# DeltaNet and a SiLU feed-forward on one core: chunk 1's inverses placed by VectorE instead of through DRAM, and GpSimd turning rows in chunks 2 to 5

## The chip, the cores and the metric

The kernel runs on one core of one Trainium2 chip. The metric is device time in microseconds (us) of one execution. The kernel before takes 667.36 us, the median of three runs (666.45, 667.36 and 670.78).

## The reference

A linear-attention block (DeltaNet) feeds a two-layer feed-forward block. There are 4 batches, 8 heads, 768 tokens and a head width of 48. All of it is fp32.

```python
k_n = k / (norm(k, axis=-1) + 1e-06)
state = zeros((B, H, D, D))
for t in range(S):
    y[:, :, t] = einsum('bhd,bhde->bhe', q[:, :, t], state)
    v_old = einsum('bhde,bhd->bhe', state, k_n[:, :, t])
    state = state + beta[:, :, t] * einsum('bhd,bhe->bhde', k_n[:, :, t], v[:, :, t] - v_old)
x = y.transpose(0, 2, 1, 3).reshape(3072, 384)
h = x @ w_in                                   # 384 -> 2048
out = (h * (1.0 / (1.0 + exp(-h)))) @ w_out    # 2048 -> 384
```

## The kernel before, in words

**Tiling.** The 768 tokens are six chunks of 128 (c = 0 to 5), and a chunk has two halves of 64 tokens (hf). The 32 pairs of batch and head are handled together, in two groups g of 16. Within a half, the recurrence is a triangular system. Its 64x64 inverse is made of 32x32 inverses on the diagonal and a corner that joins two of them. One partition holds one 32x32 inverse, so the 128 inverses of a chunk (32 pairs, four blocks of 32 tokens) fill the 128 partitions.

**One chunk.** TensorE makes the scores (`score`, L502). `block_out` (L543) sends the 32x32 diagonal blocks to DRAM and `block_in` (L550) fetches them back with one block to a partition (tile `g`). `invert` (L569) runs 31 pairs of VectorE instructions (L580, L585) on tile `x` and one final scaling (L588). Then the inverses have to come back to token-major places. In the kernel before, chunks 1 to 5 do it through DRAM: ScalarE and VectorE each turn half the rows of 64 partitions into `g` (`turn_rows`, L573, through `by_act` and `by_dve`, L517 and L520), the SP queue writes `low` and `up` to DRAM, reads `low` back as `xe` (L600) and `up` back into `xi` and `crossed` (`read_up`, L556). Chunk 0 has a way of its own, `invert_first` (L613), with two VectorE 32x32 transposes (L640, L644).

**Joins.** `solve(c)` (L922) goes on in steps: `merge(c, g, False)` (TensorE L732, reads `xe`, writes `py`, evacuated to `y` by ScalarE and VectorE), `keys` (L778, then VectorE adds into `vf`, L783), `merge(c, g, True)` (L732 into `px`, reads `xi`, `crossed` and `y`), and then for each half `inner` and `old` (L790, L856), `update` (L810), `new` (L869), and `copy_out`, which copies results to `xT` and `part`; `move` (L847) issues five DMAs `xT<-part` for each half. The scaling of `vf` by the norms (`size`, L438) is a GpSimd instruction of 128x768.

**Feed-forward.** A generator yields pieces of the previous chunk's feed-forward: `hidden` (L985, `phid`, then SiLU on ScalarE into `gT`, L995), and `project` (L1015, `po`) for chunk 0, or `combine` (L1083) for the later chunks. `combine` needs sums of quarters of `w_out`, made once by `sum_w` (VectorE L1047, eight instructions). `run(n)` puts n pieces into the order; TensorE does them while the recurrence waits.

**Order.** `pin` (L76) chains every instruction of an engine to the one before it, so each engine executes in exactly the order in which the Python code emits. The SP queue likewise takes its DMAs in order (`in_line`, L86). How much feed-forward lies between two steps of the recurrence is written out by hand: `script` texts for chunk 0 (L1421), the loops after `invert(1, step)` (L1430 to L1439), and the tuple of counts in the main loop (L1445). Weights are narrowed while they come in (`narrow`, L213: two ScalarE, two VectorE, one GpSimd instruction for a piece); `fill` (L1179) advances that, and when `eager` is set it begins the next piece at once.

`place(c, j)` (L412) says which 32 partitions token block j takes: identity for chunk 0, permuted for the others. `spread` (L312) holds the norms in these places, zero elsewhere; it is set to zero once more at L1252.

## Time and profile before

| what | value |
|---|---|
| median of three runs | 667.36 us |
| the profiled execution | 669.8 us, of it the span of instructions 668.1 us |
| TensorE matmul busy | 638.2 us (96% of the span) |
| VectorE / ScalarE / GpSimd busy | 393.0 / 215.7 / 84.3 us |
| mean granted TensorE clock | 0.969 of full speed |
| packets of the main DMA queue | 40.7% of 16 engines' span |

The profile is of one execution. A busy TensorE counts the time that matmuls are in flight, at whichever clock was granted, so a busy microsecond at half clock does half the work. In the timeline each row is a start, a duration, the engine, the line in the kernel, the operation with its output and inputs, and how many instructions were merged into the row; in brackets stands how long the engine was idle before and what ended the idle time. One `Matmult` of fp32 appears as two matmuls in these rows. SPq is the SP engine's queue, on which the DMAs are issued.

### The profile page before, as it was taken

What the parts mean: (1) busy time and instruction counts of PE and PEld (TensorE: products, weight loads), DVE (VectorE), ACT (ScalarE), POOL (GpSimd) and SP (SyncE); (2) the same over time, 40 slices, a digit from 0 to 9 for tenths busy, and PEclk for the clock granted to TensorE, in tenths of its full rate; (3) what the DMA queues carried; (4) which work ended last, traced back from release to release, by engine and by line L of the source; (5) the groups of instructions that cost most, each with busy time, mean ns of one, the idle gap of its engine ahead of it and who ended that gap; (6) DMA issues with size and microseconds to landing.
All of it is one profiled execution on the core that took longest, in us unless ns stands there. A gap on an engine that the chain in (4) does not pass through costs nothing.

```text
span 668.1 us, 21115 instructions
## 1 busy us (share of the span) xinstructions
PE 638.2 (96%) x9288; PEld 554.7 (83%) x9288; DVE 393.0 (59%) x908; ACT 215.7 (32%) x496; POOL 84.3 (13%) x86
## 2 busy tenths in 40 slices
PE   7849998998989999999999999999999999999997
PEld 5547785685778998998988998989988989989997
DVE  6845797995455796562895462977553974212112
ACT  2435685112234112452122452122452122441111
POOL 5022483500102002002001002001011000000000
PEclk9956999998889999999999999999999999999999
DMA  8991737606055816065905066715073024010101
GB/s 133 215 260 35 238 104 176 107 0 106 13 117 110 135 26 104 4 125 113 137 24 104 10 130 132 108 37 93 12 148 86 1 72 58 16 37 1 25 0 25
DMA packets 153195, 56.39 MB, mean 84 GB/s; under 512 B 124480, under 2 KB 146240, under 8 KB 153104
## 3 DMA queue, kind: packets, MB, share of 16 engines
q1 hardware_dynamic: 150656, 54.63, 40.7%
q8 instruction: 73, 1.20, 0.8%
q10 hardware_dynamic: 2448, 0.41, 0.4%
q14 instruction: 18, 0.15, 0.1%
HBM read 41.06 MB, written 11.80 MB: 79 GB/s over the span
## 4 chain that ended last, share of the span: by engine, by line
PE 54%; DVE 21%; DMA 6%; SPq 3%; issue 2%; ACT 2%; POOL 0%; DVEq 0%; ACTq 0%
PE phid L985 20%; PE px L1083 11%; PE py L1083 9%; DVE rank L580 8%; DVE x L585 7%; PE pa L502 2%; PE pz L790 2%; DVE sums_of_g L1065 2%; SPq L100 2%; PE ph L778 2%; DMA g<-blocks 2%; PE pyc L869 2%; PE pu L810 1%; PE po L1015 1%; DMA blocks<-ap 1%
## 5 line engine op out<-in xcount | busy, mean ns | idle before, releaser
L985 PE MATMUL phid<-xT,w_in 128*128 128x256 f32 x1152 | 259.8, 383 | 5.1 <-ACT gT L995 3.0
L985 PEld LDWEIGHTS phid<-xT,w_in 128*128 128x128 f32 x1152 | 216.6, 191 | 38.4 <-issue 4.6
L995 ACT ACTIVATE gT<-phid 128x512 f32<-128x512 f32 x96 | 57.0, 597 | 146.1 <-PE phid L985 139.2
L580 DVE SCALAR_TENSOR_TENSOR rank<-g,step,x 128x31 f32<-128x31 f32 (+15 forms) x155 | 63.4, 409 | 41.6 <-DMA g<-blocks 37.2
L1065 DVE TENSOR_TENSOR sums_of_g<-gT 128x384 f32<-128x384 f32 (+1 forms) x60 | 29.8, 510 | 56.4 <-ACT gT L995 45.5
L585 DVE TENSOR_TENSOR x<-x,rank 128x31 f32<-128x31 f32 (+15 forms) x155 | 55.9, 361 | 5.3
L1083 PE MATMUL px<-sums_of_w,sums_of_g 128*128 128x192 f32 x320 | 56.1, 329 | 0.0
L1083 PE MATMUL py<-w_out,sums_of_g 128*128 128x192 f32 x320 | 56.1, 329 | 0.0
L1083 PEld LDWEIGHTS px<-sums_of_w,sums_of_g 128*128 128x128 f32 x320 | 52.1, 190 | 0.5
L1083 PEld LDWEIGHTS py<-w_out,sums_of_g 128*128 128x128 f32 x320 | 52.1, 190 | 0.4
L1015 PE MATMUL po<-w_out,gT 128*128 128x384 f32 x128 | 47.1, 519 | 2.3 <-ACT gT L995 2.1
L361 POOL TENSOR_TENSOR sq<-kb 128x384 f32<-128x384 f32 x24 | 21.6, 921 | 182.1 <-DMA low<-g 130.8
L1015 PEld LDWEIGHTS po<-w_out,gT 128*128 128x128 f32 x128 | 24.3, 198 | 19.4 <-ACT gT L995 2.8
L443 POOL TENSOR_TENSOR vf<-vf,n_slot 128x768 f32<-128x768 f32 x10 | 14.6, 1475 | 157.1 <-DMA vf<-in_v_dram 157.1
L464 DVE STREAM_TRANSPOSE kq<-stage 128x512 f32<-128x512 f32 x28 | 28.4, 1121 | 8.3 <-DMA stage<-in_q_dram 7.6
L517 ACT COPY xT<-pyc 48x128 f32<-48x128 f32 (+2 forms) x126 | 32.7, 260 | 1.6
L790 PEld LDWEIGHTS pz<-vf,xi 64*64 64x64 f32 x768 | 26.9, 149 | 4.7 <-issue 3.7
L790 PE MATMUL pz<-vf,xi 64*64 64x48 f32 x768 | 28.8, 233 | 1.1 <-issue 1.1
L815 DVE TENSOR_TENSOR state<-state,pu 128x384 f32<-128x384 f32 x22 | 11.2, 550 | 30.5 <-PE pu L810 30.1
L1083 PE MATMUL py<-w_out,gT 128*128 128x192 f32 x160 | 28.1, 329 | 0.0
L1083 PE MATMUL px<-w_out,gT 128*128 128x192 f32 x160 | 28.1, 329 | 0.0
L1083 PE MATMUL px<-sums_of_w,gT 128*128 128x192 f32 x160 | 28.1, 329 | 0.0
(174 smaller groups left out, 775.3 us busy)
## 6 DMA issues: line engine op xcount, KB each, us to landing
vf<-in_v_dram SPq DMA_DIRECT2D x48, 96.0 KB, 3.2
out_dram<-o SPq DMA_DIRECT2D x46, 96.0 KB, 2.2
sums_of_w<-in_moe_w_out_dram SPq DMA_DIRECT2D x5, 768.0 KB, 5.3
w_out<-in_moe_w_in_dram SPq DMA_DIRECT2D x4, 768.0 KB, 6.3
blocks<-ap SPq DMA_DIRECT2D x44, 64.0 KB, 1.9
g<-blocks SPq DMA_DIRECT2D x5, 512.0 KB, 3.9
up<-x SPq DMA_DIRECT2D x5, 512.0 KB, 4.0
xi<-up SPq DMA_DIRECT2D x20, 128.0 KB, 3.8
```

The costliest lines, as they stand in the source:

```text
L361: pin(nc.gpsimd.tensor_tensor(out=squared[c, b // HB][:, b % HB], in0=kb, in1=kb, op=ALU.mult))
L443: pin(nc.gpsimd.tensor_tensor(out=vf, in0=vf, in1=of, op=ALU.mult))
L464: pin(nc.vector.transpose(out=kqs[c, b][:, :, j, :].rearrange("p a (i m) -> p a m i", i=T), in_=src.rearrange("p a (m d) -> p a m d", d=D) ...
L517: return pin(nc.scalar.copy(to, of))
L580: pin(nc.vector.scalar_tensor_tensor(out=tv, in0=g[:, 0:m, m : m + 1].to_broadcast([P, m, n]), scalar=step[:, m : m + 1], in1=x[:, m : m + ...
L585: yield pin(nc.vector.tensor_tensor(out=x[:, 0:m, m:T], in0=x[:, 0:m, m:T], in1=tv, op=ALU.add))
L790: yield pin(nc.tensor.matmul(pz[rows, n * D : (n + 1) * D], lhsT=xis[g][rows, u * H + 2 * p + e, :], rhs=vfs[c][rows, hf, g * HB + u, p, : ...
L985: pin(nc.tensor.matmul(ph[:, j * GT : (j + 1) * GT], lhsT=w_in[:, a, (2 * f + j) * P : (2 * f + j + 1) * P], rhs=xTs[c, hf][:, a, :], star ...
L995: pin(nc.scalar.activation(out=gTs[f // FG][:, f % FG, :], in_=ph[:], func=ACTF.Silu, scale=-0.5 if in_blocks(c) else 0.5))
L1015: pin(nc.tensor.matmul(po[n][:, 0:DM], lhsT=gTs[f // 2 // FG][:, f // 2 % FG, at : at + C], rhs=w_outs[f // HFF][:, f % HFF, :], start=(f ...
L1065: pin(nc.vector.tensor_tensor(out=sums_of_g[:, k, fs], in0=of[0], in1=of[1], op=op))
L1083: pin(nc.tensor.matmul(to, lhsT=at, rhs=quarter(f, *b) if isinstance(b, tuple) else sums_of_w[b][:, f], start=start and f == 0, stop=f == ...
```

## The change

Chunk 1 loses its way through DRAM. After the final scaling, a new function `put_up` makes two VectorE 32x32 transposes of `x`: one straight into the tile that `merge` reads (`xe`, which now shares a tile with `y`), and one into a part of `sum_tile` (at `AT_LAST`). From there copies of 32 partitions by 512 elements put the blocks into `xi` and `crossed`: two by VectorE, two by GpSimd, six by ScalarE. Chunk 1's token blocks are no longer permuted (`place`). The ten DMAs of chunk 1 for `low`, `up`, `xe`, `xi` and `crossed` are gone.

In chunks 2 to 5 the half of the row turning that ScalarE did is done by GpSimd (`by_pool`).

The joins of chunk 1 are given four pieces sooner: six pieces lie between the inverses and the first `merge` in place of ten; one of the four is moved to just behind that `merge`, three to the place behind the first half's `copy_out`. In the engines' orders this moves eight `po` matmuls on TensorE (sixteen of the profile's rows): two to behind the first merge, six to behind `new` of the first half. `sum_w` is spread over the steps of `solve(1)`, so six of its eight VectorE instructions come after joins that they preceded, and the two GpSimd scalings of chunk 1's `vf` come behind `put_up`'s copies, where they stood ahead of them in time. In the weight loading, the next piece is begun after the feed-forward piece and not before it; in the engines' orders that exchanges one SiLU (L995) with the two ScalarE instructions of one piece. The clearing of `spread` moves to behind chunk 1's `block_steps`.

```diff
--- before.py
+++ after.py
@@ -258,7 +258,8 @@
     AT_X = AT_G + (T + 1) * T
     AT_UP = AT_X + SLAB
     AT_LOW = AT_UP + BH * T
-    assert AT_LOW + BH * T // 2 <= 3 * HFF * HM
+    AT_LAST = 2 * HFF * HM
+    assert AT_LOW + BH * T // 2 <= 3 * HFF * HM and BH * T <= HFF * HM
 
     def spare_w(i):
         return sums_of_w[i].rearrange("p f m -> p (f m)").bitcast(U32)
@@ -411,7 +412,7 @@
 
     def place(c, j):
 
-        return 2 * (1 - j % 2) + j // 2 if c > 0 else j
+        return 2 * (1 - j % 2) + j // 2 if c > 1 else j
 
     EVEN = slice(W, P)
 
@@ -519,6 +520,9 @@
     def by_dve(to, of):
         return pin(nc.vector.tensor_copy(out=to, in_=of))
 
+    def by_pool(to, of):
+        return pin(nc.gpsimd.tensor_copy(out=to, in_=of))
+
     blocks = {}
 
     def block_room(c):
@@ -566,6 +570,21 @@
                     crossed[T * (4 - j) : T * (5 - j)], up[at + HH : at + T].rearrange("n s t -> s n t")
                 )
 
+    def put_up(x):
+
+        both = work.tile([P, BH, T], FP32, name="xe_y", tag="g", bufs=1)
+        xes[1], ys[1] = both[:], both[:].rearrange("p (g h) t -> p g h t", g=2)
+        pin(nc.vector.transpose(out=both[:].rearrange("p n s -> p s n"), in_=x))
+        up = sum_room[:, AT_LAST : AT_LAST + BH * T].rearrange("p (n t) -> p n t", t=T)
+        pin(nc.vector.transpose(out=up.rearrange("p n t -> p t n"), in_=x.rearrange("p s t -> p t s")))
+        for j in (1, 3, 0, 2):
+            rows, cols = slice(T * j, T * (j + 1)), slice(T * (j % 2), T * (j % 2) + T)
+            for g in range(2):
+                of = up[rows, HH * g : HH * (g + 1)]
+                if j % 2 == 1 and g == 1:
+                    by_act(crossed[T * (4 - j) : T * (5 - j)], of)
+                (by_dve if j % 2 == 1 and g == 0 else by_pool if j % 2 == 0 and g == 0 else by_act)(xis[g][rows, :, cols], of)
+
     def invert(c, step):
 
         _, g, x = blocks.pop(c)
@@ -590,7 +609,10 @@
         ))
         for _ in range(1):
             yield
-        turn_rows(by_act, slice(0, T // 2))
+        if c == 1:
+            put_up(x)
+            return
+        turn_rows(by_pool, slice(0, T // 2))
         turn_rows(by_dve, slice(T // 2, T))
         low, up = (tc.dram_tile([n, T, T], FP32, name=f"{name}{c}") for name, n in (("low", W), ("up", P)))
         issue(low[:], g[EVEN])
@@ -1168,7 +1190,12 @@
             if piece.name in names:
                 piece.begin()
 
-    eager = []
+    eager, soon = [], []
+
+    def begin_soon():
+        for piece in soon:
+            piece.begin()
+        soon.clear()
 
     def begin_next():
         for piece in queue:
@@ -1195,9 +1222,9 @@
                     ("in", 4): [0], ("in", 5): [1], ("in", 7): [5], ("out", 2): [6], ("out", 3): [7]
                 }.get(piece.name, [])
                 if eager and queue and queue[0].name in raws:
-                    queue[0].begin()
+                    soon.append(queue[0])
             elif eager and piece.done == 1 and len(queue) > 1 and queue[1].name in raws:
-                queue[1].begin()
+                soon.append(queue[1])
 
     def until(name):
         while name not in narrowed:
@@ -1249,7 +1276,6 @@
     for t in xis:
         pin(nc.gpsimd.memset(t, 0.0))
     step = block_steps(0)
-    pin(nc.gpsimd.memset(spread[:], 0.0))
     fetch_w_in(0)
     load_k(1)
     fetch_w_in(1)
@@ -1330,6 +1356,7 @@
             if name is not None:
                 until(name)
             go(pieces)
+            begin_soon()
 
     def lengths(c):
 
@@ -1394,6 +1421,7 @@
                 go(solving, n)
             elif what == "f":
                 fill(n)
+                begin_soon()
             elif what == "r":
                 run(n)
             elif what == "l":
@@ -1418,39 +1446,39 @@
     assert next(solving, 0) == 0
     load_v(1)
     ready = prepare(1)
-    script("r l6 r p r l6 f p l9 f2 r p r f2 l9 r p r f2 r")
+    script("r l6 r p r l6 f p l9 r f2 p r f2 l9 r p r f2 r")
     step = block_steps(1)
+    pin(nc.gpsimd.memset(spread[:], 0.0))
     script("f p")
     while queue:
         run()
         fill(2)
+        begin_soon()
     go(long, 99)
     load_k(2)
     inv = invert(1, step)
     for n, _ in enumerate(inv):
-        if n % 4 != 3:
-            run()
+        run(int(n % 4 != 3))
     until(("out", NWI - 1))
     sums_made = sum_w()
-    for n in range(10):
+    for n in range(6):
         run()
-        go(sums_made, int(n < 6))
-        if n in (7, 8):
-            size(1, n - 7)
+        if n in (2, 3):
+            size(1, n - 2)
     for c in range(1, NCH):
         solving = solve(c)
         long = lengths(2) if c == 1 else iter(())
         for n in range(9):
             go(solving)
-            run(((1, 1, 1, 1, 0, 3, 1, 1, 1) if c == 1 else (2, 2, 2, 2, 1, 1, 2, 2, 1))[n])
+            run(((2, 1, 1, 1, 0, 6, 1, 1, 1) if c == 1 else (2, 2, 2, 2, 1, 1, 2, 2, 1))[n])
             if n == 5:
                 if c == 1:
                     run(999)
                     needed = iter(())
                 pieces = chained(pieces, feed_forward(c, 0), feed_forward(c, 1))
             go(long, (1, 0, 1, 1, 9, 9, 9, 9, 9)[n])
-            if c == 1 and n > 5:
-                go(sums_made, 2 if n == 8 else 1)
+            if c == 1:
+                go(sums_made, (1, 1, 1, 1, 1, 1, 0, 0, 2)[n])
         assert next(solving, 0) == 0
         go(long, 99)
         if c + 1 < NCH:
```

## The prediction

> **What bounds the kernel now.** I read the busy shares first, then the clock and idle time of TensorE by stage, then the waits, then the timeline around the places that the diff names.

> ```profile
> PE 638.2 (96%) x9288; PEld 554.7 (83%) x9288; DVE 393.0 (59%) x908; ACT 215.7 (32%) x496; POOL 84.3 (13%) x86
> ```

> TensorE is in use for 638.2 of 668.1 us and the change removes none of its matmuls. So only two things can be won: its idle time (29.9 us in all) and the time at which its clock is halved. The table by stage shows both around chunk 1's joins (columns: window, its length, PE, PEld, DVE, ACT and POOL busy, granted clock, DMA share, GB/s).

> ```profile
> 160.00:170.00 10.00, 7.99 (x198) 5.75 (x199) 2.36 (x4) 1.16 (x2) 0.00 (x0) 0.62 0.79 109
> 170.00:180.00 10.00, 10.00 (x379) 6.91 (x381) 4.00 (x9) 2.18 (x5) 3.22 (x4) 0.87 0.01 3
> 180.00:190.00 10.00, 7.87 (x128) 4.82 (x122) 8.93 (x37) 2.63 (x8) 0.00 (x0) 0.98 0.18 43
> 190.00:200.00 10.00, 10.00 (x278) 8.90 (x271) 2.96 (x6) 4.45 (x13) 0.00 (x0) 0.85 0.74 148
> ```

> TensorE idles 2.0 us at 160 and 2.1 us near 187. As the clock is either 1.0 or 0.5, a mean of c over 10 us is 20(1-c) us at half: 7.6 + 2.6 + 0.4 + 3.0 = 13.6 us, whose cost is at most half, 6.8 us. Each stretch begins behind one of the gaps. The timeline says what the gaps wait for:

> ```profile
> 148.21 11.77 PE L1015 MATMUL po<-w_out,gT 128*128 128x384 f32 x36
> 161.02 0.25 PE L732 MATMUL py<-xe,ap 32*32 32x32 f32 x4 [1.04 <-DMA xe<-low]
> 162.26 1.90 PE L732 MATMUL py<-xe,ap 32*32 32x32 f32 x124 [0.99 <-DMA xe<-low]
> 164.09 2.93 PE L1015 MATMUL po<-w_out,gT 128*128 128x384 f32 x4
> 188.36 1.28 PE L985 MATMUL phid<-xT,w_in 128*128 128x256 f32 x4 [1.96 <-DMA xT<-part]
> ...
> 151.67 1.23 DVE L588 TENSOR_TENSOR x<-x,step 128x1024 f32<-128x1024 f32 x1
> ```

> The inverses are ready at 152.9 and their way through DRAM lasts to 162.26: that is the first gap. The second waits for the five DMAs `xT<-part`. A `po` row takes 0.33 us (11.77/36) at full clock, 0.73 (2.93/4) at half.

> In chunks 3 to 5 the same tail costs otherwise: ScalarE stands in order before its half of the row turning, and the SiLU behind it holds TensorE up.

> ```profile
> PE phid L985 <- ACT gT L995: 3.0, 3, 1.6
> ...
> 349.71 1.08 ACT L517 COPY g<-x 64x512 f32<-64x512 f32 x1 [4.39 <-DVE x L588]
> 351.47 8.04 PE L985 MATMUL phid<-xT,w_in 128*128 128x256 f32 x36 [1.60 <-ACT gT L995]
> ```

> **Part 1: chunk 1's inverses without DRAM.** Added on the path are VectorE's transposes. The first feeds the merge.

> ```profile
> L640 DVE STREAM_TRANSPOSE sums_of_w<-sums_of_w 128x512 f32<-128x512 f32 x1 | 1.1, 1060 | 0.0
> L644 DVE STREAM_TRANSPOSE sums_of_w<-sums_of_w 128x1024 f32<-128x1024 f32 x1 | 1.9, 1943 | 0.0
> ...
> 124.65 1.40 DVE L580 SCALAR_TENSOR_TENSOR rank<-g,step,x 128x60 f32<-128x60 f32 x1
> 126.09 1.40 DVE L585 TENSOR_TENSOR x<-x,rank 128x60 f32<-128x60 f32 x1
> 127.53 0.31 DVE L580 SCALAR_TENSOR_TENSOR rank<-g,step,x 128x87 f32<-128x87 f32 x1
> 124.50 2.91 POOL L443 TENSOR_TENSOR vf<-vf,n_slot 128x768 f32<-128x768 f32 x2
> ```

> The rows from 124.65 show a side effect. Two VectorE instructions of 128x60 take 1.40 us where the larger one of 128x87 takes 0.31, and each ends as one of GpSimd's two `vf` scalings (1.46 us each) ends. The change gives those scalings behind the copies, so the inverse is done about 2 x 1.09 = 2.2 us sooner, at 150.7. Two transposes, 2.1 (two of L640) and 1.9 us, put `xe` at 152.8 and the second copy of the inverses at 154.7.

> TensorE reaches the merge sooner too: sixteen `po` rows (5.2 us) move behind it, so it comes at 160.0 - 5.2 = 154.8. `xe` is 2.0 us early, and the first gap closes. The ten DMAs of the old way leave the SP queue, behind which only two stores of `o` stand.

> **What is late next** is ScalarE: six copies of 32x512 before the SiLU that the last two `po` matmuls of chunk 0 need.

> ```profile
> L517 ACT COPY y<-py 32x512 f32<-32x512 f32 x10 | 5.8, 578 | 7.9 <-PE py L732 7.8
> L517 ACT COPY g<-x 64x512 f32<-64x512 f32 x5 | 5.5, 1104 | 18.5 <-DVE x L588 18.5
> ```

> No row has these copies from SBUF to SBUF. The bounds are 0.58 us (a 32x512 copy with rows in sequence) and 1.10 (one read across rows). They read in sequence, so I take 0.58: ScalarE is through at 158.2, the SiLU at 158.8, its two `y` copies at 160.0. TensorE does the merge (1.3 us), eight rows of `po` (2.6, to 158.7) and `keys` (1.1), needs the SiLU at 159.8 and `y` after four more rows at 161.1. One microsecond of room in both. GpSimd's scalings now end at about 159 (two copies, then 2.9 us from 156), just ahead of the end of `keys`; behind them VectorE has the `vf` adds and one `sum_w` (0.95 us) before the second merge ends at 162.3. I cost this at nothing; without the cover it is 1 us.

> **The second gap** gets twelve more `po` rows, 3.9 us, in front of the `phid` that waited 1.96. `part` on VectorE comes one `sum_w` later:

> ```profile
> L1047 DVE TENSOR_TENSOR sums_of_w<-w_out 128x768 f32<-128x768 f32 x2 | 1.8, 954 | 0.0
> 182.81 0.68 DVE L520 COPY part<-pyc 48x512 f32<-48x512 f32 x1 [0.37 <-ACT xT L517]
> ```

> That is 0.95 less the 0.37 it waits anyway, 0.6 us, and the DMAs follow. 3.9 - 1.96 - 0.6 leaves 1.3 us of room. The gap closes.

> **The clock.** With no gap of 2 us left in the stage, I let both halved stretches go. `po` and `phid` rows lose the full half, the small matmuls less (the first merge: 1.90 us against 1.29 in chunk 3, quoted below), so I take 6.3 of the 6.8 us. [...]

> **The weight loading.** The SiLU exchanged with two ScalarE instructions frees a gap of 2.14 us, but the weights then set the pace:

> ```profile
> 100.00:150.00 50.00, 47.73 (x237) 33.64 (x236) 44.44 (x98) 14.89 (x28) 15.14 (x10) 1.00 0.46 95
> ...
> 105.02 2.20 PE L1015 MATMUL po<-w_out,gT 128*128 128x384 f32 x6 [2.14 <-ACT gT L995]
> 111.01 16.43 PE L1015 MATMUL po<-w_out,gT 128*128 128x384 f32 x48
> 122.71 1.83 POOL L230 TENSOR_TENSOR w_out<-w_out,sums_of_w 128x768 int32<-128x768 int32 x1 [0.95 <-issue]
> ```

> The last eight of the 48 rows need GpSimd's last piece, ready at 124.5; they started at 127.4 - 2.6 = 124.8. So 0.2 us comes through.

> TensorE is thus 2.0 + 2.1 + 6.3 + 0.2 = 10.6 us sooner when chunk 1 is done.

> **Part 2: how much of it reaches chunk 2, and chunks 2 to 5.** The next inverse hangs on the SP queue, which is full from the query loads to the block DMAs:

> ```profile
> 190.72 6.91 SPq L156 DMA_DIRECT2D stage<-in_q_dram  x12
> 208.47 4.27 SPq L100 DMA_DIRECT2D blocks<-ap  x8
> 257.31 0.92 SPq L600 DMA_DIRECT2D xe<-low  x2
> 260.44 1.52 PE L732 MATMUL py<-xe,ap 32*32 32x32 f32 x128
> ```

> It starts at 190.72; of the half clock of 190 to 200 (3.0 us) 2.3 us lie after that, 1.0 us of gain that the queue doesn't share. So chunk 2's `xe` comes 9.6 us sooner while TensorE comes 10.6 sooner, and before the two were level (the merge took 1.52 us in place of 1.29, its second operand late). I count 9.6.

> The landings of `xe` in all chunks, and the issues and merges of chunks 3 to 5:

> ```profile
> DMA to landing us min/median/max: 2.3/3.0/3.1
> ...
> 355.42 0.92 SPq L600 DMA_DIRECT2D xe<-low  x2
> 359.44 1.29 PE L732 MATMUL py<-xe,ap 32*32 32x32 f32 x128
> 453.49 0.92 SPq L600 DMA_DIRECT2D xe<-low  x2
> 457.51 1.29 PE L732 MATMUL py<-xe,ap 32*32 32x32 f32 x128
> 550.94 0.93 SPq L600 DMA_DIRECT2D xe<-low  x2
> 554.93 1.29 PE L732 MATMUL py<-xe,ap 32*32 32x32 f32 x128
> ```

> With the SiLU free, TensorE's 3.0 us of waiting goes, but it then stands before `xe`. The second of each pair is issued 0.46 us after the first and lands at most 3.1 later: 359.0, 457.05, 554.5, which is 0.46, 0.46 and 0.43 before the merges that ran. Only 1.35 of the 3.0 us come through.

> The chain also has GpSimd's copy now. Nearest rows: 0.63 us for its copy of 128x512 (below), 1.10 for ScalarE's copy of the same shape. I take 1.10, no change, as the read across rows doubled ScalarE's time. At 0.63 the chains shorten by 0.47 each until TensorE binds (about 1.5 us in all); at twice 0.63 they lengthen by 0.16 each. [...]

> ```profile
> L641 POOL COPY sums_of_w<-pick x1: 632/632/632, 29.6 to 29.6; 128x512 f32<-128x512 f32 x1
> ```

> **The sum.** 9.6 + 1.35 = 11.0 us off the profiled execution's 669.8 gives 658.8. The median of before is 2.4 lower than that execution. If executions differ in the halved stretches, which go, 658.8 stands; if elsewhere, it is 656.4. Nothing shown decides; I take the middle, 657.6.

> **The rivals** (each with the same 1.2 us off).

> *The DMA leaves room.* If `xe` lands sooner because the queue is emptier or GpSimd is quick, all of 10.6 and 3.0 us come through: 669.8 - 13.6 - 1.2 = 655.0. Against it: all ten landings of `xe` took 2.3 to 3.1 us.

> *ScalarE blocks.* At 1.10 us a copy the SiLU ends 3.1 us later, at 161.9, and TensorE waits 2.1 us at `po`; a gap that long halved the clock here, for 3 to 10 us, 1.4 to 5 us more. Total loss 3.5 to 7: 661 to 664.7, say 663. For it: the order is fixed and ScalarE's copies can be twice as slow; against it: their reads are in sequence.

> *The halving isn't the gaps'.* Were the half clock to come regardless, only 4.3 us go in chunk 1 and 1.35 later: 669.8 - 5.7 - 1.2 = 662.9. For it: the gap of 2.14 us at 102.9 was followed by no halving (the clock is 1.00 in the whole stretch from 100 to 150).

> *GpSimd's turning is slow, and the kernel slower.* It stands in all four chains, and each microsecond over 1.10 costs 4 us. From 3.9 us a copy the gain is gone; at 5.5 the time is above 674. Against it: 0.63 us for as many elements, and GpSimd is idle there.

> **How the numbers follow.** Forecast 0.60, *room* 0.15, *ScalarE blocks* 0.13, *not the gaps'* 0.07, *GpSimd slow* 0.03, anything else 0.02. The low end is 656.4 less 1.5 and something for *room*: 653.5. The high end takes in *ScalarE blocks* at its middle: 663.0. About 1% (6.7 us) is what a measurement of this kernel tells from no change, a time of 660.7. Below it are nearly all of the forecast and *room*: 0.75. *ScalarE blocks* and *not the gaps'* lie within 1%: 0.21. Slower by over 1%: 0.04.

> **What would show it.** Right: no `xe<-low` in chunk 1; first merge near 155 with no idle time before it; clock 1.0 from 150 to 200; `phid` of chunks 3 to 5 no longer waiting for `gT`, and the merges waiting under 1.2 us for `xe<-low`; `g<-x` on GpSimd near 1.1 us. Wrong: `po` waiting for `gT` near 160, a clock of 0.5 there, or `xe` landing later than 10.3 us behind the inverse (now 359.0 - 349.7 = 9.3).

## The result and the profile after

The changed kernel takes 665.62 us, the median of 16 runs (660.37 to 671.65); the kernel before took 670.82 us beside it (16 runs, 666.33 to 674.04). The ratio is 0.9919, with a 95% interval of 0.9893 to 0.9945. So it is faster by 0.8%, and 8.0 us slower than forecast. Its profiled execution took 665.58 us. Ratios, and the means further down, are taken over those executions that lie within 1.5% of the same kernel's fastest (14 of the changed kernel's 16).

First the lines that answer to those of the prediction: busy time from the page, then the stages around chunk 1's joins from the table by stage (columns as in the prediction).

```profile
PE 635.3 (96%) x9288; PEld 554.2 (84%) x9288; DVE 397.2 (60%) x911; ACT 214.3 (32%) x497; POOL 92.4 (14%) x92
```

```profile
150.00:160.00 10.00, 10.00 (x278) 6.28 (x278) 9.13 (x10) 5.84 (x10) 4.46 (x4) 1.00 0.01 3
160.00:170.00 10.00, 9.03 (x355) 6.73 (x342) 6.78 (x15) 2.91 (x8) 3.86 (x4) 1.00 0.11 25
170.00:180.00 10.00, 10.00 (x109) 6.32 (x111) 8.72 (x32) 1.99 (x7) 0.00 (x0) 1.00 0.16 40
180.00:190.00 10.00, 8.53 (x278) 7.29 (x270) 3.43 (x7) 4.05 (x12) 0.00 (x0) 1.00 0.74 151
190.00:200.00 10.00, 10.00 (x162) 8.81 (x160) 7.24 (x13) 5.17 (x16) 3.35 (x3) 1.00 0.54 102
450.00:460.00 10.00, 7.06 (x215) 6.38 (x215) 7.35 (x26) 0.64 (x2) 0.00 (x0) 0.97 0.15 22
460.00:470.00 10.00, 10.00 (x170) 9.43 (x168) 2.91 (x5) 2.51 (x6) 0.00 (x0) 0.69 0.01 3
```

The clock is 1.00 all through chunk 1's joins, as forecast. But a new place shows up: from 450 to 470, in chunk 4, TensorE idles 2.9 us and the clock falls to 0.69. The timeline of the changed kernel shows chunk 1's new way, and then, engine by engine (TensorE, VectorE), what happens in chunk 4.

```profile
147.50 1.22 DVE L607 TENSOR_TENSOR x<-x,step 128x1024 f32<-128x1024 f32 x1
148.75 1.96 DVE L577 STREAM_TRANSPOSE xe_y<-x 128x1024 f32<-128x1024 f32 x1
150.57 1.90 DVE L579 STREAM_TRANSPOSE sums_of_w<-x 128x1024 f32<-128x1024 f32 x1
152.51 0.62 ACT L518 COPY crossed<-sums_of_w 32x512 f32<-32x512 f32 x1 [7.89 <-DVE sums_of_w L579]
...
152.54 1.61 POOL L524 COPY xi<-sums_of_w 32x512 f32<-32x512 f32 x2 [29.85 <-DVE sums_of_w L579]
...
152.89 1.29 PE L754 MATMUL py<-xe_y,ap 32*32 32x32 f32 x128
156.28 0.60 ACT L1017 ACTIVATE gT<-phid 128x512 f32<-128x512 f32 x1
```

```profile
448.87 2.87 PE L1105 MATMUL px<-w_out,gT 128*128 128x192 f32 x16
451.67 1.15 PE L800 MATMUL ph<-state,kq 48*64 48x48 f32 x64
452.74 2.87 PE L1105 MATMUL px<-sums_of_w,gT 128*128 128x192 f32 x16
...
456.23 0.18 PE L754 MATMUL px<-crossed,y 32*32 32x32 f32 x1 [0.44 <-DVE y L521]
...
459.87 0.20 PE L754 MATMUL px<-crossed,y 32*32 32x32 f32 x1 [2.50 <-issue]
```

```profile
449.26 0.18 DVE L390 SCALAR_TENSOR_TENSOR nr<-nt,seed 128x32 f32<-128x32 f32 x1
...
454.33 0.23 DVE L410 COPY n_slot<-n 64x8 f32<-64x8 f32 x2
454.57 1.40 DVE L521 COPY y<-py 32x512 f32<-32x512 f32 x2
```

Chunk 1's first merge starts at 152.89 with no wait for a DMA; nothing of ScalarE's copies or the SiLU at 156.28 holds TensorE up. In chunk 4 the second merge (`px`) first waits 0.44 us for VectorE's half of `y`, which comes late because the norm steps of the next chunk (the rows from 449.26 to 454.33) stand ahead of it in VectorE's order. Then, after 115 of its 128 matmul rows, TensorE stops for 2.50 us with "issue" as the cause: nothing that the profile names holds it.

Another part of the page bears on it: a DMA queue that carries instructions (columns: packets, MB, share).

```profile
q8 instruction: 73, 1.20, 0.8%
```

That is 73 packets of 16 KB. TensorE has 2 x 9288 instructions, 254 for each packet, and the stops fit this. From 150 us on, the changed kernel has five of over 0.4 us with "issue" as the cause, ending at 164.83, 182.25, 186.80, 369.60 and 459.87; they end at the 5314th, 6081st, 6337th, 11457th and 13761st of TensorE's instructions (its waits counted in), so they stand multiples of 256 apart, to within one. From these counts I take it that TensorE's instructions come in blocks of 256, one packet a block. A merge is such a block's length (128 matmuls and 128 weight loads), done in 1.3 us. The DMA view of the changed kernel has no packet of q8 from 453 to 457.1, and one from 457.1 to 459.8, here the first row; the second is the kernel before, where the packet of the same block lies between 463.3 and 465.3, before its `px` at 465.40. In the trace's record of single packets, that of the changed kernel goes out at 457.18 and has landed at 458.32.

```profile
q8 instruction: 1, 0.02, 2.7%
```

```profile
q8 instruction: 1, 0.02, 3.9%
```

So the fetch of the next block went out only 0.95 us after TensorE had passed its wait for `y` (at 456.23), near the end of the block that it was running through, and TensorE stood still until 1.5 us after the landing. Most fetches go without such a stop: 56 of the 73 packets go out from 150 us on, against the five stops.

### The profile page after: what moved, and what is told of

The parts are those of the page before. It is cut to its first block, busy times and chain, and to the rows that moved or that the text cites. A ratio compares the mean times of both kernels' runs of the same rounds, so it can differ in the third digit from the quotient of the medians.

```text
span 663.4 us, 21117 instructions
## 1 busy us (share of the span) xinstructions
PE 635.3 (96%) x9288; PEld 554.2 (84%) x9288; DVE 397.2 (60%) x911; ACT 214.3 (32%) x497; POOL 92.4 (14%) x92
## 4 chain that ended last, share of the span: by engine, by line
PE 56%; DVE 18%; DMA 5%; issue 4%; SPq 2%; POOL 1%; ACT 1%; DVEq 0%; POOLq 0%; ACTq 0%
PE phid L1007 21%; PE px L1105 10%; PE py L1105 9%; DVE rank L599 5%; DVE x L604 5%; PE po L1037 4%; PE pz L812 2%; DVE sums_of_g L1087 2%; PE pa L503 2%; PE pyc L891 2%; PE pu L832 1%; PE ph L800 1%; DMA up<-x 1%; SPq L100 1%; DMA g<-blocks 1%
## 5 line engine op out<-in xcount | busy, mean ns | idle before, releaser
L1105 PE MATMUL py<-w_out,sums_of_g 128*128 128x192 f32 x320 | 58.7, 339 | 0.0
L1105 PEld LDWEIGHTS py<-w_out,sums_of_g 128*128 128x128 f32 x320 | 54.5, 197 | 0.5
L1037 PE MATMUL po<-w_out,gT 128*128 128x384 f32 x128 | 44.5, 495 | 2.7 <-POOL w_out L230 1.8
L444 POOL TENSOR_TENSOR vf<-vf,n_slot 128x768 f32<-128x768 f32 x10 | 14.6, 1475 | 160.4 <-DVE ap L513 89.2
L524 POOL COPY g<-x 64x512 f32<-64x512 f32 x4 | 5.8, 1462 | 156.0 <-DVE x L607 156.0
```

What stands on the lines that cost most here:

```text
L444: pin(nc.gpsimd.tensor_tensor(out=vf, in0=vf, in1=of, op=ALU.mult))
L1037: pin(nc.tensor.matmul(po[n][:, 0:DM], lhsT=gTs[f // 2 // FG][:, f // 2 % FG, at : at + C], rhs=w_outs[f // HFF][:, f % HFF, :], start=(f ...
L1105: pin(nc.tensor.matmul(to, lhsT=at, rhs=quarter(f, *b) if isinstance(b, tuple) else sums_of_w[b][:, f], start=start and f == 0, stop=f == ...
```

## The experiments

Stretches at half clock come and go between executions (13.65, 0, 3.41 and 6.83 us of them from 150 to 200 in four profiles of the kernel before), so a time alone says little. Every run gives its span and its mean granted clock, and I take span times clock as an estimate of the time that the same work would take at full clock (for stretches in which TensorE sets the pace; a `po` row took 0.33 us at full clock and 0.73 at half); the rest of the span is then what the half clock cost. For the first profile of before that is 668.1 x 0.969 = 647.4 us, and 20.7 us for the clock. I call the two "full-clock time" and "clock loss". Means, with twice their standard error:

| kernel | executions | full-clock us | clock loss us | ratio to before, 95% interval |
|---|---|---|---|---|
| before (three groups) | 7, 20, 21 | 652.0, 652.2, 651.7 (each ±1.1 or less) | 17.7, 16.9, 16.9 | 1 |
| after | 14 | 648.1 ±0.8 | 14.8 | 0.9919 (0.9893 to 0.9945) |
| c1_only | 4 | 648.2 ±1.6 | 14.8 | 0.9898 (0.9848 to 0.9947) |
| pool_only | 10 | 652.9 ±1.4 | 19.4 | 1.0049 (1.0012 to 1.0085) |
| joins_late | 10 | 650.9 ±1.0 | 16.1 | 0.9965 (0.9932 to 0.9998) |
| dve_rows | 4 | 646.3 ±2.1 | 13.0 | 0.983 (0.9764 to 0.9896) |
| shift | 4 | 648.4 ±2.5 | 14.6 | 0.99 (0.9852 to 0.9947) |
| norms_later | 4 | 644.3 ±0.5 | 15.4 | 0.9851 (0.9782 to 0.9919) |
| both | 6 | 644.7 ±1.1 | 13.9 | 0.9837 (0.9794 to 0.9879) |
| before_norms | 9 | 648.9 ±1.9 | 15.8 | 0.9924 (0.9885 to 0.9962) |
| pool_norms | 10 | 648.5 ±1.4 | 17.1 | 0.9961 (0.9923 to 1.0) |
| c1_norms | 4 | 645.3 ±1.5 | 11.7 | 0.983 (0.9764 to 0.9895) |
| before_one | 9 | 651.3 ±1.6 | 16.6 | 0.9988 (0.9953 to 1.0022) |

The first four runs weigh three theories on the gap in chunk 4. A: GpSimd's copy of 1.46 us delays VectorE, so `y` is late, TensorE waits for it just ahead of a block's edge, and the fetch comes late. B: the place of the edge alone does it. C: a late DMA of `xi` or `crossed` does it.

### Chunk 1's part alone

```diff
-        turn_rows(by_pool, slice(0, T // 2))
+        turn_rows(by_act, slice(0, T // 2))
```

> Chunk 1's part alone: in chunks 2 to 5 ScalarE turns the rows again, in place of GpSimd. Theory A (GpSimd's 1.46 us copy makes the norms and with them VectorE's copy of y late; TensorE waits 0.44 us for y ahead of chunk 4's second merge, stands in that wait with the edge of an instruction block just ahead, so that the next block is fetched late: 2.5 us without work, and then two windows at half clock): y is in time, no gap of 2.5 us in chunk 4, no half clock behind 200 us; phid waits for gT again, about 3.0 us in chunks 3 to 5; time about 0.989 of before. Theory B (the edge of the instruction block alone makes the gap; the new kernel's stream has two more instructions ahead of it): the gap of 2.5 us and the half clock stay, time about 0.998 of before. Theory C (the DMAs xi and crossed land too late for the second merge): no gap, as TensorE comes later; about 0.989.

The gap in chunk 4 is there without GpSimd's turning, in this run's timeline:

```profile
458.27 0.18 PE L754 MATMUL px<-crossed,y 32*32 32x32 f32 x1
...
461.79 0.18 PE L754 MATMUL px<-crossed,y 32*32 32x32 f32 x1 [2.38 <-issue]
```

TensorE did not even idle for `y` here; it arrived just as `y` was done (458.01). So GpSimd's slow copy, my first suspect, is not needed for the gap. Half clock (3.41 us) follows the gap here too, and `phid` waits for the SiLU 0.95 us in chunks 3 to 5, not the 3.0 us that I expected. In time this kernel is as fast as the whole change: GpSimd's part brings nothing that can be seen.

### VectorE turns all rows

```diff
-        turn_rows(by_pool, slice(0, T // 2))
-        turn_rows(by_dve, slice(T // 2, T))
+        turn_rows(by_dve, slice(0, T))
```

> The changed kernel, with VectorE turning all rows of chunks 2 to 5 in one instruction of 64x1024, neither GpSimd nor ScalarE. A: the turning takes about 1.25 us where GpSimd's half takes 1.46, low is issued some 0.25 us sooner behind the inverse, y is in time or late by under 0.2 us; no gap of 2.5 us; time about 0.984 of before. B: the gap in chunk 4 stays; about 0.992. C: the gap shrinks by 0.25 us at most; about 0.992.

The wait for `y` (0.48 us) and the gap (2.50 us, at 457.33) stay. One copy of all rows, 64x1024, takes 1.06 us and so beats GpSimd's 1.46 us for half of them; the mean is 1.8 us better at full clock, but with four executions on this side the error is over 2 us. The ratio, 0.983, is close to the 0.984 that A named, though the gap is still there.

### TensorE's instructions moved by 128 places

```diff
+    def tiny(n):
+        pw = bank(CC, "pw")
+        for _ in range(n):
+            pin(nc.tensor.matmul(pw[0:T, 0:T], lhsT=ident[0:T, 0:T], rhs=ident[0:T, 0:T], start=True, stop=True))
...
     pin(nc.gpsimd.memset(spread[:], 0.0))
+    tiny(32)
```

> The changed kernel, with 32 matmuls of 32x32 more ahead of chunk 1's last scores, which nothing reads: 128 more instructions on TensorE, half a block of 256, so that every edge of a block behind them lies elsewhere. They cost about 0.8 us, where TensorE waits for weights anyway. A and B: the wait of 0.44 us for y in chunk 4 stays, the gap of 2.5 us behind it goes, and the gaps of 0.86 and 0.82 us without a cause in chunk 1 go or stand elsewhere; time about 0.984 of before. C: the gap of 2.5 us stays where it is; about 0.992.

The gap left chunk 4 and came up in chunk 3, while the wait for `y` stayed in chunk 4. First row chunk 3, second row chunk 4 of this run's timeline:

```profile
361.38 0.18 PE L759 MATMUL px<-crossed,y 32*32 32x32 f32 x1 [2.58 <-issue]
```

```profile
461.10 0.18 PE L759 MATMUL px<-crossed,y 32*32 32x32 f32 x1 [0.46 <-DVE y L526]
```

The three shorter stops of chunk 1 (0.86, 0.65 and 0.82 us in the changed kernel) went as well, but for 0.23 us, and chunk 1 took 65.6 us in place of 68.6 (between the two matmuls named further down). The ratio, 0.990, is not the 0.984 that A and B had named, as the long gap only moved. So the long gap hangs on where the edges between blocks of 256 instructions lie, and a late `y` alone costs its 0.46 us and no more. No run had a wait for a DMA of `xi` or `crossed` at this place, so C falls.

### The norm steps given later

```diff
-        long = lengths(2) if c == 1 else iter(())
+        long = lengths(2) if c == 1 else after
...
-            go(long, (1, 0, 1, 1, 9, 9, 9, 9, 9)[n])
+            go(long, (1, 0, 1, 1, 9, 9, 9, 9, 9)[n] if c == 1 else (0, 0, 3, 3, 3, 9, 9, 9, 9)[n])
...
-                go(after, 2)
-            go(after, 99)
+                go(after)
```

> The changed kernel, with the later part of the norms of chunks 3 to 5 behind the merges in place of ahead of them on VectorE, so that its copy of y comes at once. A: no wait for y, no gap of 2.5 us, no half clock behind 200 us; time about 0.984 of before. B: the gap of 2.5 us stays (the edge of the block is where it was); about 0.992. C: the gap stays, as the DMAs are as before; about 0.992.

With fewer norm steps ahead of it, `y` is copied from 450.33 on and done at 451.73; TensorE comes to `px` at 454.72 and stops for 0.41 us instead of 2.50:

```profile
450.33 1.40 DVE L521 COPY y<-py 32x512 f32<-32x512 f32 x2
```

```profile
456.30 0.18 PE L754 MATMUL px<-crossed,y 32*32 32x32 f32 x1 [0.41 <-issue]
```

At full clock it is 3.8 us below the changed kernel, and no clock loss after the start is left but at the very end.

### GpSimd's part alone

```diff
+    def by_pool(to, of):
+        return pin(nc.gpsimd.tensor_copy(out=to, in_=of))
...
-        turn_rows(by_act, slice(0, T // 2))
+        turn_rows(by_pool if c > 1 else by_act, slice(0, T // 2))
```

> The kernel before with GpSimd's row turning in chunks 2 to 5 and nothing else; chunk 1 keeps its way through DRAM. Edge-and-late-y theory: chunk 1 is untouched, so the block edges of TensorE's instructions stand where they stood in before, chunk 4's px merge has no 2.5 us gap even though GpSimd's copy takes 1.46 us; the 3.0 us of waits for the SiLU go and about as much returns as waits for xe (0.3 to 1.0 us a chunk), ratio to before 0.995 to 1.000. Rival (GpSimd's slow copy is what makes the gap): a gap of 2 to 2.5 us and 3.4 us or more of half clock stand in chunk 4 here too, ratio 1.003 to 1.010.

Here I was wrong: TensorE runs exactly before's instructions in before's order, so its blocks lie where they lay, and still the gap came, as the rival had it.

```profile
464.88 0.18 PE L735 MATMUL px<-crossed,y 32*32 32x32 f32 x1 [0.38 <-DVE y L520]
...
468.25 0.21 PE L735 MATMUL px<-xi,y 32*32 32x32 f32 x1 [2.21 <-issue]
```

The SiLU no longer holds TensorE up, TensorE reaches the merges sooner relative to VectorE, and `y`, which in before was done just in time, is late. The edge need not move for the gap to come. In time this kernel is 0.5% slower than before, with an interval (1.0012 to 1.0085) that leaves out 1.

### Both edits of before and after crossed with the norm steps

The late norm steps were put on the kernel before, on GpSimd's part alone, and on chunk 1's part alone (`by_act` in place of `by_pool`), with the same lines as above.

> The kernel before with the norm steps of chunks 3 to 5 given one a piece and late, and nothing else. By full-clock time (span times mean granted clock; 652.0 us for before). Theory (the edit only cures a late y, and in before y stands 0.15 us ahead of TensorE): nothing to cure, 651.5 to 652.5, ratio 0.997 to 1.003. Rival (VectorE's norm steps cost time by their place in every chunk): 649 to 651, ratio 0.993 to 0.997.

> The kernel before with GpSimd's row turning in chunks 2 to 5 and the late norm steps; chunk 1 as in before. TensorE's program holds the same instructions as in before. Theory (y late by 0.38 us is what brings the 2.21 us gap in chunk 4 when the block edges stand as in before): no idle time for y and no gap over 0.6 us at chunk 4's px; full-clock time 652.9 - 2.6 = 650.3, within 649.5 to 651, ratio to before 0.993 to 0.999. Rival (the gap has another cause than the late y): a gap of 2 us or more stays there, 652.5 to 653.5, ratio 1.001 to 1.008.

> The changed kernel with the late norm steps, and ScalarE turning rows again in chunks 2 to 5, so against the run with late norm steps it undoes GpSimd's part alone (that one: full-clock time 644.3). Theory (with y cured GpSimd's copies are worth the 3.0 us of waits for the SiLU less 1.8 us of waits for xe): 645 to 646.5, ratio to before 0.985 to 0.991, and the waits for the SiLU stand again in chunks 3 to 5. Rival (GpSimd's 1.46 us give it all back): 643.8 to 644.8, ratio 0.980 to 0.986.

With norms_later all eight combinations of three parts (chunk 1's, GpSimd's and the norm steps) have been run, and full-clock times compare them. Chunk 1's part gives 652.0 - 648.2, 652.9 - 648.1, 648.9 - 645.3 and 648.5 - 644.3: 3.8, 4.8, 3.6 and 4.2 us, whatever else is in the kernel. GpSimd's part gives -0.9, 0.1, 0.4 and 1.0 us, each within its error of some 2 us. The norm steps give 3.1, 4.4, 2.9 and 3.8 us (errors 1.0 to 2.2). So pool_norms went as the theory had it and somewhat beyond (its gap is down to 0.39 us); c1_norms lies at the lower edge of its theory by full-clock time and in the rival's range by its ratio, which does not settle what GpSimd is worth once `y` is early. And before_norms was a surprise: I had said that in before there was nothing to cure, since its profile shows no gap in chunk 4; yet it gained 3.1 us, just past the fast edge of what the rival had.

### One tiny matmul in the kernel before

```diff
     step = block_steps(1)
+    tiny(1)
     script("f p")
```

> The kernel before with one matmul of 32x32 (four of the profile's TensorE rows, into a bank that nobody reads) ahead of the last scores of chunk 1, so that every later instruction of TensorE stands four places further in its blocks of 256. Theory (the place of the edge matters by itself, as chunk 1's rewrite alone, with y no later than in before, showed a gap of 2.38 us): chunk 4's px shows a gap of 2 us or more though y is there as early as in before; full-clock time 652.0 + 2.4 = 654.4, within 653.5 to 655, ratio 1.002 to 1.009. Rival (only a late y brings the gap): no gap over 0.6 us there, 651.5 to 652.5, ratio 0.997 to 1.003.

Its profile has the gap, as the theory had it, but the time did not move, as the rival had it:

```profile
466.44 0.18 PE L737 MATMUL px<-crossed,y 32*32 32x32 f32 x1 [2.14 <-issue]
```

The two agree only if before itself has this gap in many executions. That put the first profile in question.

### The kernel before, and the one after, profiled again

> The kernel before unchanged, profiled once more, to see which parts of the first profile belong to the kernel and which to that execution (its full-clock time, 668.1 x 0.969 = 647.4 us, is 4.6 below the mean of 652.0). Theory (the first profile was a lucky one in chunk 4 and an unlucky one in chunk 1): in at least two of the three new profiles chunk 4's px has a gap of 2 us or more, and the half clock between 150 and 200 is 0 to 6.8 us where the first showed 13.65. Rival (the first profile is typical): no such gap in any of the three, and 10 to 14 us of half clock there.

> The same again: the kernel before, unchanged. Theory: a gap of 2 us or more at chunk 4's px in at least two of three, half clock between 150 and 200 of 0 to 6.8 us. Rival: no gap, 10 to 14 us.

> The changed kernel unchanged, profiled once more. Theory: no half clock between 150 and 200 again, and the gap of 2.3 to 2.6 us at chunk 4's px again, as y is late there by construction. Rival (that gap is chance too): no gap over 0.6 us there.

(The third of these profiles of before, before_again2, had the same expectation.) Two of the three have the gap: the first row is before_again1, the second before_again3.

```profile
464.17 0.21 PE L732 MATMUL px<-xi,y 32*32 32x32 f32 x1 [2.75 <-issue]
```

```profile
468.38 0.18 PE L732 MATMUL px<-xi,y 32*32 32x32 f32 x1 [2.21 <-issue]
```

before_again2 has none. The clock around chunk 1's joins differs as much; from the table by stage, before_again1 (no half clock at all) and before_again3 (two half windows of 3.41 us):

```profile
160.00:170.00 10.00, 7.93 (x316) 5.29 (x301) 3.60 (x6) 2.31 (x4) 1.11 (x2) 1.00 0.57 71
...
180.00:190.00 10.00, 7.94 (x247) 5.72 (x248) 6.83 (x25) 2.00 (x5) 0.00 (x0) 1.00 0.40 93
190.00:200.00 10.00, 9.76 (x205) 8.65 (x197) 7.05 (x10) 5.81 (x19) 0.00 (x0) 1.00 0.85 153
```

```profile
160.00:170.00 10.00, 6.76 (x202) 4.11 (x200) 2.40 (x4) 1.16 (x2) 0.00 (x0) 0.92 0.82 115
180.00:190.00 10.00, 7.98 (x108) 4.59 (x105) 8.96 (x34) 2.63 (x8) 0.00 (x0) 0.94 0.18 43
190.00:200.00 10.00, 9.73 (x279) 8.63 (x272) 2.29 (x5) 4.55 (x13) 0.00 (x0) 0.89 0.76 148
```

The idle time there is as large as in the first profile or larger, but the half clock is 0, 3.41 and 6.83 us in the three, where the first had 13.65. The theory holds: the first profile was lucky in chunk 4 and unlucky in chunk 1. The changed kernel's gap is steady: its second profile waits 0.45 us for `y` and then stands 2.77 us.

```profile
457.95 0.18 PE L754 MATMUL px<-crossed,y 32*32 32x32 f32 x1 [0.45 <-DVE y L521]
...
461.86 0.18 PE L754 MATMUL px<-crossed,y 32*32 32x32 f32 x1 [2.77 <-issue]
```

Put side by side, the profiles with the edge in chunk 4's `px` give a rule. Where TensorE waits for `y` (after, after_again, pool_only, joins_late, dve_rows, weights_at_once: 0.25 to 0.84 us), the gap of 2.2 to 2.8 us follows, six of six. Where `y` is done less than 0.15 us ahead of TensorE (before, its three repetitions, c1_only, before_one), it comes in four of six. Where `y` is 2.7 to 3.5 us ahead (the five with late norm steps), it never does; at most 0.41 us is left. The fetch itself tells the cases apart without exception. In the ten profiles with the long stop in chunk 4 the packet of the next block goes out 1.1 to 2.2 us after `px` has begun; in the seven others with the edge in this `px` it goes out 1.0 to 2.3 us before. In all twelve stops there, the two short ones included, TensorE goes on 2.3 to 3.0 us after the packet went out. What sends it out late was not found: TensorE waited for `y` in six of the ten, but in before and before_again2 it went out about 2 us before `y` was done.

The price can be read as well. From the first merge of chunk 4 to that of chunk 5, the eight profiles without the long stop there take 96.5 to 97.5 us and the ten with it 100.0 to 104.1: 5.1 us more in the mean, with the half clock that follows.

### The joins of chunk 1 as late as in before

```diff
-    for n in range(6):
+    for n in range(10):
         run()
...
-            run(((2, 1, 1, 1, 0, 6, 1, 1, 1) if c == 1 else (2, 2, 2, 2, 1, 1, 2, 2, 1))[n])
+            run(((1, 1, 1, 1, 0, 3, 1, 1, 1) if c == 1 else (2, 2, 2, 2, 1, 1, 2, 2, 1))[n])
```

(`sum_w` and `size` go back to their places in before as well.)

> The changed kernel with before's order of the joins of chunk 1: ten pieces ahead of the first merge, before's counts in the main loop and before's places of the sums of w_out. Theory (both gaps of chunk 1 have separate causes): the first gap (1.04 and 0.99 us for xe, and the half clock behind it) stays away because the way through DRAM is gone; the second, 1.96 us of phid waiting for xT, comes back, 1.5 to 2.2 us, with one or two half windows (3.41 or 6.83 us) behind it. Chunk 1 then gives 2 to 5 us less than in the changed kernel, ratio to before 0.994 to 1.000 if chunk 4's gap stands where it did. Rival (the joins' new places bring nothing): no wait for xT over 1 us, ratio as after, 0.992.

The theory holds: the first gap stays away, the second is back, with one half window of the clock behind it (the mean clock is 0.83 from 180 to 190).

```profile
158.49 2.85 PE L1037 MATMUL po<-w_out,gT 128*128 128x384 f32 x8 [1.42 <-ACT gT L1017]
...
183.38 1.87 PE L1007 MATMUL phid<-xT,w_in 128*128 128x256 f32 x4 [2.19 <-DVE n_slot L410]
```

The row names VectorE for the second wait, but the last of the DMAs `xT<-part` is issued in the stretch of 3.05 us from 179.50 on, so they are the likelier cause; that is not shown. The first row is the wait for the SiLU that I had as a rival (*ScalarE blocks*): in this order the SiLU stands directly behind ScalarE's six copies (154.05 to 157.81) and TensorE waits for it 1.42 us; in the changed kernel's order it doesn't wait.

### The weights begun at once

```diff
-                    soon.append(queue[0])
+                    queue[0].begin()
...
-                soon.append(queue[1])
+                queue[1].begin()
```

(With the script text as in before.)

> The changed kernel with the pieces of weights begun at once, as in before: one SiLU behind the two ScalarE instructions of a piece again. Theory (my step of +0.2 us should have been -0.6): TensorE's wait for that SiLU is 2.1 us again near 103 and the wait for the weights near 117 (1.84 us) goes; the merge of chunk 1 comes 0.3 to 0.9 us sooner relative to the same matmul at 50 us. Rival (the step as forecast, +0.2): it comes 0.2 us later or level. The total time is not told by this run beyond 1%: 660 to 668.

The changed kernel's two waits in the weight loading are the first two rows, that of this run the third:

```profile
101.14 2.20 PE L1037 MATMUL po<-w_out,gT 128*128 128x384 f32 x6 [0.66 <-ACT gT L1017]
...
116.96 8.31 PE L1037 MATMUL po<-w_out,gT 128*128 128x384 f32 x23 [1.84 <-POOL w_out L230]
```

```profile
108.76 3.50 PE L1037 MATMUL po<-w_out,gT 128*128 128x384 f32 x6 [1.87 <-ACT gT L1017]
```

2.50 us of waiting against 1.87: the exchange turns one wait into another that is 0.4 to 0.6 us longer (before had 2.14). The merge of chunk 1 comes 101.0 us after the same matmul near 50 us, against 102.9 and 101.8 in the two profiles of the changed kernel: sooner, as the theory had it, by 0.8 to 1.9 us. The one time, 672.04 us, lies outside the 660 to 668 that I had given.

### Two edits together

The norm steps of norms_later and the row turning of dve_rows.

> The changed kernel with two edits together: VectorE turns all rows in chunks 2 to 5, and chunk 2 to 5's norm steps are given one a piece and late. Theory (late y at a block edge makes chunk 4's loss, and it is cured by later norms; VectorE's turning saves about 0.5 us a chain): no 2.5 us gap in chunks 2 to 5, no half clock there, 657 to 661 us, ratio to before 0.978 to 0.985. Rival (each edit gains only by where it happens to put the block edges): a gap of 2 us or more with a halved stretch returns in some chunk, ratio 0.988 to 0.994.

No gap of 2 us and no half clock after 124 us but at the very end; 660.55 us. It is not faster than norms_later (659.85 us) or c1_norms (659.14 us): once `y` is early, which engine turns the rows no longer shows. All three beat the kernel before. Against the changed kernel, by ratio, the interval of both lies below its (0.9879 against 0.9893), that of c1_norms just touches it and that of norms_later overlaps it; at full clock all three lie 2.8 to 3.8 us below it, more than their errors.

## Why the prediction was wrong, by its own steps

**Right.** No way through DRAM; first merge at 152.89 without a wait for a DMA; both gaps of chunk 1 closed; clock 1.00 from 150 to 200; the side effect of GpSimd's scalings on VectorE (counted from the `phid` behind the weights, the final scaling starts 2.3 us sooner than in the first profile of before; 2.2 forecast); ScalarE's copies at 0.62 us, near the 0.58 taken; the SiLU and `y` of chunk 1 in time; no more waits for `gT` in chunks 3 to 5, and waits for `xe` under 1.2 us in their place (0.26 in chunk 2, 0.18 and 0.86 in chunk 3):

```profile
349.73 1.25 PE L754 MATMUL py<-xe,ap 32*32 32x32 f32 x124 [0.86 <-DMA xe<-low]
```

**The clock: 6.3 us was mis-sized.** I read 13.6 us of half clock off one execution and took nearly all of its price as a gain. Eight profiles have before's chunk 1 (the first, the three repetitions, pool_only, before_norms, pool_norms, before_one): 13.65, 0, 3.41, 6.83, 0, 6.82, 0 and 6.83 us of half clock from 150 to 200, 4.7 in the mean, which is worth 2.3 us at most. The cause was right (gaps go and halving goes with them, in all nine profiles of the new order), the size was off by 4.0 us. The rival *the halving isn't the gaps'* was wrong on the cause, but right that a gap of 2 us need not bring it. Which gaps are followed by it is a draw of each execution: in each of the eighteen profiles, all halved stretches begin a whole number of 3.41 us after the first one, and that one begins at 36.02, 36.73, 36.47 and 38.63 us in the four of before. That should have been a term of the sum.

The traces also show what the draw hangs on. Cut each of the eighteen spans into such windows of 3.41 us, from 62 to 655 us. A window at full clock in which TensorE idled 1.87 us or more was followed by half clock in 19 of 19 cases, one with less than 1.19 us in none, and between the two in 5 of 30. A gap of 2 us costs when it falls into one window, as the two waits for `xe` in the first profile did (2.03 us between 158.90 and 162.31). It cost nothing where the edge of a window split it: pool_norms idled 2.36 us up to 183.03, at most 1.52 us of it in one window, and stayed at full clock.

**The rest of chunk 1.** Between the same two matmuls (a `phid` behind the weights, at 127.38 in the first profile, and a `pa` of chunk 2, at 203.68) chunk 1 took 76.3 us in the first profile, 73.6, 74.7 and 75.7 in the other three of before, 68.6 and 68.2 in the two of after. That is 6.7 us in the mean, where 9.4 had been forecast (the 9.6 less 0.2 for the weights, which lie ahead of this `phid`). joins_late, with before's order of the joins, took 72.1 in its one profile: about 3 us of the gain are then the way through DRAM, and the rest is the new order. Against the first profile, TensorE also has stops of 0.86, 0.65 and 0.82 us at block edges (at 164.83, 182.25 and 186.80), which I hadn't foreseen; but other executions of before have them too, such as this row of before_again1:

```profile
164.51 0.92 PE L778 MATMUL ph<-state,stage 48*64 48x48 f32 x48 [1.69 <-issue]
```

**The weights: +0.2 became -0.4**, as shown above. I had looked only at the last of GpSimd's pieces, ready at 124.5; TensorE stood still for an earlier one, 1.84 us up to 116.96.

**GpSimd's copy: 1.10 became 1.46 us**, above both of my bounds (0.63 and 1.26). By the prediction's own 4 us for each microsecond over 1.10, that takes back 1.4 us.

```profile
L524 POOL COPY g<-x 64x512 f32<-64x512 f32 x4 | 5.8, 1462 | 156.0 <-DVE x L607 156.0
```

**Chunks 2 to 5: +1.35 was the step that failed in kind.** I asked what comes late behind the SiLU and named the landing of `xe`. I did not ask about the second merge, though the rows were there in the first profile:

```profile
463.93 1.39 DVE L520 COPY y<-py 32x512 f32<-32x512 f32 x2
465.40 0.24 PE L732 MATMUL px<-xi,y 32*32 32x32 f32 x2
```

There `y` ends at 465.32 and `px` starts at 465.40. A margin of 0.1 us was the cover, and TensorE gained more than that. Behind it stood the fetch of the next block, which I did not know as a cost (2.50 us in the changed kernel). From that `pa` to the end of the span the four profiles of before take 464.4, 469.2, 464.6 and 468.3 us, the two of after 469.3 and 467.9: about 2 us lost in the mean, though with a scatter as large; chunk 4's stop is in both of after, and in two of four of before.

The waits after 200 us show why even the 1.35 us did not come. Where ScalarE turns rows (eight profiles), `phid` waits for the SiLU 0.95 to 3.01 us, 1.9 in the mean, so the 3.0 us that I started from was a high draw. Where GpSimd turns them (eight others), the merges wait for `xe` and `y` 1.5 to 3.1 us, 2.1 in the mean. One wait was exchanged for another as long.

**The base.** I started from 668.6 us, halfway between the profiled execution and the median of three runs. Sixteen runs gave 670.8; 2.2 us of the miss are that.

Together, 2.2 from the base, 0.6 from the weights, 2.7 from chunk 1 and 3.3 from the rest make 8.8, against a miss of 8.0. As means of four and of two profiles they can't be expected to agree better.

## What to carry to other kernels

One profile is one draw: where a gain is read from halved clock or from stops that the profile does not explain, compare span times clock over all runs first, and profile the same kernel again before pricing it. When a wait of TensorE goes, look at every later wait whose cover was thinner than what TensorE gains, the evacuations by VectorE and ScalarE above all. And where a burst of small matmuls starts with a wait, have its operand ready some microseconds ahead: in the five profiles where it was 2.7 to 3.5 us ahead, TensorE never stopped for the next 256 instructions there for more than 0.41 us.
